# Sharing PSUM pairs between the Vh tiles, and placing the rank-32 additions ahead of the layer-norm statistics

## The chip, the cores and the metric

The kernel runs on one core of a Trainium2 chip. The metric is the device time of one execution in microseconds (us). Five engines work side by side, each through its own queue of instructions in order: TensorE (PE, matrix products, with the weight loads listed apart as PEld), VectorE (DVE), ScalarE (ACT), GpSimd (POOL) and SyncE (SP), which issues the DMAs. They meet through semaphores. PE writes into PSUM, the accumulation memory of eight banks; the other engines read it from there.

## The reference

Eight batches of attention with a feature-wise softmax, a gated MLP on top of it (`_moe_ref`), then a second one that mixes along the sequence at rank 32 and along the channels (`_moe2_ref`):

```python
# q_s, k_s: softmax of q over the features, of k over the sequence
kv = np.einsum('bhsd,bhse->bhde', k_s, v)
x = np.einsum('bhsd,bhde->bhse', q_s, kv)          # [8, 576, 512] after the transpose
h = gelu(x @ w_in); u, v = h[..., :512], h[..., 512:]
v_n = (v - mean(v)) / np.sqrt(var(v) + 1e-06) * g_ln
v_s = np.einsum('ts,bsd->btd', w_sg, v_n) + b_sg[None, :, None]
x = x + (u * v_s) @ w_out
...
h = xt @ U @ V                                     # rank 32, xt is x transposed
u = x + h.transpose(0, 2, 1)
out = u + np.maximum(u @ w_ch1, 0.0) @ w_ch2
```

## The kernel before

Products are made from a high and a low part of each operand (names ending in `h` and `l`; the low part is made by a subtraction that the helper `low` puts on DVE or POOL, and all subtractions and additions of that kind bear line L55). The helper `mm` (L52) issues all matrix products. The program has a loop over eight batches b = 0 to 7 and then, from 631.9 us of the span on, a long phase of channel products (tiles `mm`) which is PE from end to end and which the change doesn't touch.

One batch goes through these stages, in PE's order:

- **Vh.** Five tiles `pv` (`emit_Vh`): four of 12 matmuls and 128 rows, and tile 4 with 8 matmuls and 64 rows. ACT applies GELU to each into a buffer `ge` (three buffers), DVE makes `bn_stats` and `bn_aggr` (`stats`), POOL raises the variance to the power -1/2. `emit_ln` then makes a shift `sh` on DVE (L620), applies it on ACT (L623, `ge<-ge,sh,mv`), copies it to `vh` on ACT, and makes the low part `vl` on POOL; for tile 4 the low part is made on DVE, into the other half of the tile `vh4`.
- Between these tiles stand products of the batch before: transposes of its result (`emit_yT`, tile `pt`), the rank-32 product with U (`emit_U`, `pp`), and the rank-32 additions (`emit_PV`: tiles `pw`, added on DVE as `yt<-pw,yt`, and sent out by SP as `u2d<-yt`).
- **Uh.** Four tiles `pu` (`emit_Uh`), to each of which ACT applies GELU (L645, `ut<-pu`). The buffer of `ut` is that of `yt`, so the first `ut` waits for the four `u2d` transfers. Beside this DVE and ACT prepare the softmax of the next batch: on DVE `q_sub` (`qt<-qt,qm`), `k_sub` (`kt<-kt,pb`), then `q_sum` and `q_norm`; on ACT the exponentials (L458 for q, L439 for k). The exponential and GELU need different function tables, and an `ACT_TABLE_LOAD` stands wherever ACT goes from one to the other.
- **S.** Four tiles `pS` (`emit_S`): the first needs `vh4` at its end. DVE makes `gt<-pS,gl,bb` (L665) and `gt<-gt,ut`; `split_G` makes `gh` and `gl`.
- **pk, pt, y, px.** The product `pk` of keys and values, transposes of q (`emit_qT`, low part `ql` on DVE), the output product `py` (`emit_y`, which needs all four `gt` and, by its PSUM buffers, the reads of `gt` and `ql`), and `px`, the x of the next batch.

PSUM is shared by two pools: `big`, three buffers of two banks each, and `ps1`, two buffers of one bank each. In the kernel before each `pv` takes a whole `big` buffer though it fills one bank, as do the tiles `pw`, the transposes of tiles 2 and 3 of the batch before, `pu`, `pS`, `py` and `px`.

PE's order and, inside the batches, DVE's order are those in which the code is written (`in_order`). ACT, POOL and SP are put in order by a scheduler when the program is built. `slot` puts work on the weights of the later phase (`chw`, `f`, `stg`) at fixed places. A wait for a tile is a wait for the whole tile: two halves of one tile are one thing to those waits when their reader and the next writer are different engines.

Of the kernel before, what the change touches and what calls it, by code (L numbers as in the profile page):

```python
# [8 lines left out]
F32 = mybir.dt.float32  # L9
# [3 lines left out]
ALU = mybir.AluOpType  # L13
# [9 lines left out]
def fused_kernel(tc, q, k, v, w_in, g_ln, w_sgT, b_sg, w_out, U, V, w_ch1, w_ch2, outT):  # L23
    nc = tc.nc
    B, S, C = q.shape
    P = 128
    H, D = 8, 64
    NT = S // P
    R = S - NT * P
    NC = C // P  # L30
    F = w_out.shape[0]
# [17 lines left out]
    pe, act, dve, pool, sp = nc.tensor, nc.scalar, nc.vector, nc.gpsimd, nc.sync  # L49

    def mm(out, lhsT, rhs, first, last, onto=False):
        pe.matmul(out, lhsT, rhs, start=first, stop=last, skip_group_check=onto)  # L52

    def tt(eng, out, a, b, op):
        return eng.tensor_tensor(out=out, in0=a, in1=b, op=op)  # L55
# [4 lines left out]
    def copy(out, src):  # L60
        return act.activation(out, src, AF.Copy)  # L61

    def low(eng, out, src, hi):
        return tt(eng, out, src, as_f32(hi), ALU.subtract)

    def opened(name, bufs=1, **kw):
        cm = tc.tile_pool(name=name, bufs=bufs, reuse_waits="tile", **kw)
        return cm.__enter__(), lambda: cm.__exit__(None, None, None)
# [8 lines left out]
    ps2, close_ps2 = opened("ps2", 3, space=PSUM)  # L77
    ps1, close_ps1 = opened("ps1", 2, space=PSUM)
# [4 lines left out]
    wrk, close_wrk = opened("wrk", side="left")  # L83
    wo_p, close_wo = opened("wo_p", side="left")
    sg_p, close_sg = opened("sg_p", side="left")
    tmpp, close_tmpp = opened("tmpp", 2, side="left")
# [10 lines left out]
    half = cst.tile([P, 1], F32, name="half")  # L97
# [326 lines left out]
    def k_spread(b):  # L424

        mx = kx_t[b]
        pb = ps1.tile([P, NC, P], F32, tag="ps1", name="pb")
        for c in range(NC):
            pe.transpose(pb[:, c], mx[:, c : c + 1].to_broadcast([P, P]), ident)
        kx_t[b] = pb.rearrange("p c e -> p (c e)")  # L430
# [15 lines left out]
    def q_max(b, t):  # L446
        if t == 0:
            q_s[b] = tmpp.tile([P, NT + 1, H], F32, tag="qm", name="qm")
        dve.tensor_reduce(
            out=q_s[b][0 : TR[t], t], in_=q3(t), op=ALU.max, axis=mybir.AxisListType.X  # L450
        )
# [79 lines left out]
    def halves(t):  # L531
        return t[:, :, 0:HS]

    def two(ap):
        return ap.rearrange("p (j n) -> p j n", n=HS)
# [10 lines left out]
    def behind(eng):  # L546
        return tc.issue_after(last[eng].ins)
# [31 lines left out]

    vh = {}  # L580
    ln = {}

    def emit_Vh(b, t):
        xh, xl, xr, _ = x_t[b]
        pv = ps2.tile([P, 1024], F32, tag="big", name="pv")[:, 0:F]
        wv_h, wv_l = wi[1]
        for kc in range(NC):
            if t < NT:
                a, l = xh[:, kc, t * P : (t + 1) * P], xl[:, kc, t * P : (t + 1) * P]
                mm(pv, a, wv_h[:, kc], kc == 0, False)  # L590
                mm(pv, a, wv_l[:, kc], False, False)
                mm(pv, l, wv_h[:, kc], False, kc == NC - 1)
            else:
                a = xr[:, kc].rearrange("p j r -> p (j r)")
                mm(pv, a, wv_h[:, kc], kc == 0, False)
                mm(pv, a, wv_l[:, kc], False, kc == NC - 1)
        ge = tmpp.tile([P, F], F32, tag="ge", name="ge", bufs=3)
        ln[b, t] = ge
        if t < NT:
            act.activation(ge, pv, AF.Gelu_apprx_tanh)  # L600
        else:
            copy(ge[0:R], pv[64 : 64 + R])
            tt(dve, ge[0:R], pv[0:R], ge[0:R], ALU.add)
            act.activation(ge[0:R], ge[0:R], AF.Gelu_apprx_tanh)
# [11 lines left out]
    def emit_ln(b, t):  # L616
        ge, mv = ln.pop((b, t))
        n = TR[t]
        shift = tmpp.tile([P, 1], F32, tag="sh", name="sh", bufs=4)
        dve.scalar_tensor_tensor(  # L620
            out=shift[0:n], in0=mv[0:n, 0:1], scalar=-1.0, in1=mv[0:n, 1:2], op0=ALU.mult, op1=ALU.mult
        )
        act.activation(ge[0:n], ge[0:n], AF.Identity, bias=shift[0:n], scale=mv[0:n, 1:2])  # L623
        h = wrk.tile([P, F], F32R, tag=f"vh{t}", name=f"vh{t}")
        if t < NT:
            l = wrk.tile([P, F], F32R, tag=f"vl{t}", name=f"vl{t}")
            copy(h, ge)
            low(pool, l, ge, h)
            vh[b, t] = (h, l)
        else:  # L630
            copy(h[0:R], ge[0:R])
            low(dve, h[64 : 64 + R], ge[0:R], h[0:R])
            vh[b, t] = h
# [57 lines left out]
    def emit_yT(b, t):  # L691
        n = TR[t]
        if t not in (2, 3) or b == B - 1:
            pt = ps1.tile([P, C], F32, tag="ps1", name="pt1")
        else:
            pt = ps2.tile([P, 1024], F32, tag="big", name="pt1")[:, 0:C]
        for c in range(NC):
            pe.transpose(pt[0:n, c * P : (c + 1) * P], y_t[b][:, c, t * P : t * P + n], ident)  # L698
        h = wrk.tile([P, C], F32R, tag=f"vh{t}", name=f"yh{t}")
        if t < NT:  # L700
            l = wrk.tile([P, C], F32R, tag=f"vl{t}", name=f"yl{t}")
            copy(h, pt)
            low(dve, l, pt, h)
            yn[b, t] = (h, l)
        else:
            copy(h[0:R], pt[0:R])
            low(dve, h[64 : 64 + R], pt[0:R], h[0:R])
            yn[b, t] = (h,)
# [31 lines left out]
    def emit_PV(b, c):  # L740
        s = pu_t[b][:, c * P : (c + 1) * P]
        pw = ps2.tile([P, 2, 512], F32, tag="big", name="pw")
        for j in range(2):
            mm(pw[:, j, 0:HS], s, v_w[:, j * HS : (j + 1) * HS], True, True)
        y = y_t[b][:, c]
        tt(dve, two(y), halves(pw), two(y), ALU.add)
        sp.dma_start(u2d[:, c, :, b * HS : (b + 1) * HS].rearrange("j p n -> p j n"), two(y))
# [26 lines left out]
    def u_parts(g, kc):  # L774

        n, t0 = GROUPS[g], starts[g]
        if kc == 0:
            parts = [tmpp.tile([P, F], F32, tag="ge", name="us", bufs=3) for _ in range(3)]
            parts.append(wrk.tile([P, F], F32, tag="xr", name="us3"))
        else:  # L780
            parts = [wrk.tile([P, F], F32, tag=x, name="us") for x in ("vh0", "vl0", "vh1", "vl1")]
        parts = [t[:, 0:n] for t in parts]
        for x, t in enumerate(parts):
            sp.dma_start(t, u2d[x % 2, kc + 2 * (x // 2), :, t0 : t0 + n])
        return parts
# [103 lines left out]
    us = {}  # L889
# [364 lines left out]
    for b in range(B):  # L1254
# [12 lines left out]
            load_ahead()  # L1267
        for t in range(NT + 1):
            emit_Vh(b, t)
            if nxt:  # L1270
                with behind(dve):
                    for t2 in Q_MAX[b > 0][t]:
                        q_max(nxt, t2)
                    for _ in range(FOLDS[b > 0][t]):
                        next(fold)
            if t < NT:
                stats(b, t)
            slot(TURNS[b][0][t])
            if t > 0:
                emit_ln(b, t - 1)  # L1280
            if t == NT:
                stats(b, t)
            if b > 0:
                for t2 in ((2,), (3, 4), (), (), ())[t]:
                    emit_yT(b - 1, t2)
            if t == 2 and b > 0:
                for t2 in range(NT + 1):
                    emit_U(b - 1, t2)
            if b > 0:
                for c in ((), (), (), (0, 1), (2, 3))[t]:  # L1290
                    emit_PV(b - 1, c)

        spread_at = 2 if b else 3
        if nxt:
# [13 lines left out]
        for f in range(NF):  # L1308
            if nxt and f == spread_at:
                k_spread(nxt)  # L1310
            if b == 0:
                slot(TURNS[b][1][f])
            if not nxt:
                for _ in range((0, 2, 2, 2)[f]):
                    next(prep, None)
            emit_Uh(b, f)
            if f == 0:
                emit_ln(b, NT)
                if nxt:
                    load_v(nxt)  # L1320
                else:
                    next(prep, None)
            if nxt:
                for t in Q_SUB[b > 0][f]:
                    q_sub(nxt, t, pool if t in Q_SUB_POOL[b > 0] else dve)
                for t in K_SUB[b > 0][f]:
                    if f >= spread_at:
                        k_sub(nxt, t)
                    else:
                        late_k.append(t)  # L1330
                if f == spread_at:
                    for t in late_k:
                        k_sub(nxt, t)
            if b > 0:
                slot(TURNS[b][1][f])
# [181 lines left out]
```

## Time and profile before

| | |
|---|---|
| times of three runs | 1308.29, 1314.53 and 1307.48 us, median 1308.29 |
| the profiled execution | 1311.05 us, of which the span is 1309.2 us |
| mean granted TensorE clock | 0.991 |
| PE busy | 1260.0 us, 96% |
| DVE busy | 969.0 us, 74% |
| ACT busy | 636.9 us, 49% |
| POOL busy | 330.4 us, 25% |
| chain that ended last | PE 79%, DVE 7%, DMA 4%, ACT 2% |

A busy share is an average over the whole span. The stages differ: the batches 1 to 6 take some 69 to 73 us each, the first and the last batch 116 and 97 us, and the phase behind them 677 us. In a row of the timeline a bracket at the end, such as [0.21 <-ACT ge L600], is the idle time of that engine just before the row and what ended it. Successive instructions of one kind are one row with xN, and their time is that of all of them.

### The profile page before, as it was taken

The numbers are of one execution on the slowest core, as the hardware profiler recorded it, in microseconds if no ns is written. First come the engines' busy times: TensorE is split into PE (matmuls) and PEld (weight loads), VectorE is DVE, ScalarE is ACT, GpSimd is POOL, SyncE is SP. The second block draws the span as 40 slices with busy tenths as digits, with TensorE's granted clock in tenths as the row PEclk, the third lists the DMA queues.
The fourth block names the chain that finished last, engine by engine and source line by source line (L and its number), as shares of the span: only waits on it lengthen the run. The fifth ranks groups of instructions, "written<-read, shape, count | busy, mean of one in ns | idle before, by whom it ended". The sixth has DMA issues, their size and how long they took to land.

```text
span 1309.2 us, 20581 instructions
## 1 busy us (share of the span) xinstructions
PE 1260.0 (96%) x7592; PEld 1139.1 (87%) x7592; DVE 969.0 (74%) x1406; ACT 636.9 (49%) x979; POOL 330.4 (25%) x426
## 2 busy tenths in 40 slices
PE   4799999999999999898999999999999999999998
PEld 3598999999898989798888888888888889999998
DVE  7888879787988888788668953598337963694485
ACT  4756656575757466654454512444134422451342
POOL 4634152624243333665340202000010002000000
PEclk9899999999999999998999999999999999999999
DMA  8515171725343352468998667678756788899896
GB/s 268 164 47 171 37 218 37 225 70 167 96 151 120 111 168 73 162 208 299 312 344 315 227 231 257 209 242 290 257 193 226 243 285 297 269 304 315 260 290 215
DMA packets 135907, 274.14 MB, mean 209 GB/s; under 512 B 15232, under 2 KB 56704, under 8 KB 135808
## 3 DMA queue, kind: packets, MB, share of 16 engines
q1 hardware_dynamic: 135808, 272.84, 63.2%
q8 instruction: 60, 0.98, 0.3%
q14 instruction: 39, 0.32, 0.1%
HBM read 224.56 MB, written 48.23 MB: 208 GB/s over the span
## 4 chain that ended last, share of the span: by engine, by line
PE 79%; DVE 7%; DMA 4%; ACT 2%; issue 1%; POOL 1%; SPq 0%; DVEq 0%; ACTq 0%; POOLq 0%
PE mm L52 50%; PE pS L52 6%; PE pu L52 6%; PE pv L52 5%; PE py L52 5%; DMA stg<-in_w_ch_dram 1%; PE pm L52 1%; PE pp L52 1%; PE px L52 1%; PE pt L698 1%; DVE yt L55 1%; DVE f L183 1%; PE pk L52 1%; PE pt L527 1%; DMA wu<-wd 1%
## 5 line engine op out<-in xcount | busy, mean ns | idle before, releaser
L52 PE MATMUL mm<-oh,wu 128*128 128x512 f32 (+1 forms) x1120 | 320.7, 367 | 0.0
L52 PE MATMUL mm<-uh,wu 128*128 128x512 f32 (+1 forms) x1064 | 303.7, 366 | 1.9 <-DMA wu<-wd 1.1
L52 PEld LDWEIGHTS mm<-oh,wu 128*128 128x128 f32 x1120 | 207.0, 188 | 26.1
L52 PEld LDWEIGHTS mm<-uh,wu 128*128 128x128 f32 x1064 | 196.3, 188 | 26.4 <-issue 1.4
L52 PE MATMUL mm<-ol,wu 128*128 128x512 f32 (+1 forms) x560 | 205.7, 367 | 0.0
L61 ACT ACTIVATE oh<-h 128x1024 fp32r<-128x1024 f32 (+1 forms) x140 | 135.2, 973 | 124.8 <-PE mm L52 102.4
L52 PE MATMUL mm<-ul,wu 128*128 128x512 f32 (+1 forms) x532 | 194.9, 366 | 0.0
L55 DVE TENSOR_TENSOR ol<-h,oh 128x1024 fp32r<-128x1024 f32 (+1 forms) x140 | 155.4, 1113 | 40.9 <-ACT oh L61 40.1
L55 POOL TENSOR_TENSOR ust<-ust 128x1024 f32<-128x1024 f32 (+1 forms) x16 | 36.4, 2282 | 389.4 <-DMA ust<-u2d 348.8
L55 DVE TENSOR_TENSOR h<-mm,u 128x1024 f32<-128x1024 f32 (+1 forms) x57 | 63.3, 1111 | 87.8 <-PE mm L52 87.7
L52 PEld LDWEIGHTS mm<-ol,wu 128*128 128x128 f32 x560 | 105.2, 188 | 13.1
L55 DVE TENSOR_TENSOR u<-mm,u 128x1024 f32<-128x1024 f32 (+1 forms) x53 | 58.9, 1111 | 76.7 <-PE mm L52 71.3
L52 PEld LDWEIGHTS mm<-ul,wu 128*128 128x128 f32 x532 | 99.9, 188 | 12.1
L55 POOL TENSOR_TENSOR chw<-f,chw 128x256 fp32r<-128x256 f32 x98 | 78.9, 820 | 95.4 <-ACT chw L61 95.3
L55 DVE TENSOR_TENSOR h<-h,h 128x1024 f32<-128x1024 f32 (+1 forms) x80 | 88.9, 1112 | 0.0
L1041 ACT ACTIVATE h<-mm 128x1024 f32<-128x1024 f32 (+1 forms) x19 | 17.8, 938 | 130.8 <-PE mm L52 130.8
L1032 ACT ACTIVATE h<-h 128x1024 f32<-128x1024 f32 (+1 forms) x60 | 58.1, 969 | 33.9 <-DVE h L55 33.9
L61 ACT ACTIVATE chw<-f 128x256 fp32r<-128x256 f32 x112 | 42.6, 412 | 62.7 <-DVE f L184 23.1
L61 ACT ACTIVATE u<-mm 128x1024 f32<-128x1024 f32 (+1 forms) x24 | 22.5, 939 | 103.1 <-PE mm L52 86.9
L171 POOL TENSOR_SCALAR stg<-stg 128x256 f32<-128x256 f32 (+1 forms) x83 | 41.0, 496 | 99.7 <-DMA stg<-in_w_ch_dram 39.0
L52 PE MATMUL py<-gh,wo_h 128*128 128x288 f32 x256 | 57.6, 307 | 3.0 <-DVE gt L665 2.1
L52 PE MATMUL py<-gl,wo_h 128*128 128x288 f32 x256 | 56.0, 301 | 3.4 <-DVE gl L55 3.4
(165 smaller groups left out, 2650.2 us busy)
## 6 DMA issues: line engine op xcount, KB each, us to landing
wu<-wd SPq DMA_DIRECT2D x280, 512.0 KB, 4.4
wd<-chw SPq DMA_DIRECT2D x112, 256.0 KB, 3.6
stg<-in_w_ch_dram SPq DMA_DIRECT2D x64, 256.0 KB, 3.7
u2d<-yt SPq DMA_DIRECT2D x32, 288.0 KB, 2.4
vt<-in_v_dram SPq DMA_DIRECT2D x32, 256.0 KB, 6.7
qt<-in_q_dram SPq DMA_DIRECT2D x7, 1024.0 KB, 8.1
kt<-in_k_dram SPq DMA_DIRECT2D x7, 1024.0 KB, 6.1
res<-u2d SPq DMA_DIRECT2D x12, 512.0 KB, 5.3
```

The lines of the kernel that those rows point to most:

```text
L52: pe.matmul(out, lhsT, rhs, start=first, stop=last, skip_group_check=onto)
L55: return eng.tensor_tensor(out=out, in0=a, in1=b, op=op)
L61: return act.activation(out, src, AF.Copy)
L171: eng.tensor_scalar(out=hi, in0=hi, scalar1=F64_MOST, scalar2=-F64_MOST, op0=ALU.min, op1=ALU.max)
L183: dve.tensor_scalar(out=b, in0=b, scalar1=3, scalar2=None, op0=ALU.logical_shift_left)
L527: pe.transpose(pt[:, t * P : (t + 1) * P], qt[:, t, c * P : (c + 1) * P], ident)
L698: pe.transpose(pt[0:n, c * P : (c + 1) * P], y_t[b][:, c, t * P : t * P + n], ident)
L1032: act.activation(h, h, AF.Relu)
L1041: act.activation(h_out(j, 11, n), bank, AF.Relu)
```

## The change

From batch 1 on the tiles `pv` 0 and 1 share one `big` buffer, one bank each, and so do 2 and 3 (`half_pair`). Tile 4 takes a buffer of `ps1`. The transposes of tiles 2 and 3 of the batch before share one as well. The GELU is taken out of `emit_Vh` into `gelu_Vh`, so that from tile 3 on the rank-32 additions of the batch before (`emit_PV`) are written ahead of the GELU and the statistics of that tile. The shift `sh` becomes a `tensor_scalar` whose scalar is a pointer to the variance term. The layer norm of tile 4 is written behind Uh 1 in place of Uh 0. In the preparation of the last phase two buffers change places.

```diff
+    def half_pair(key, half, name):
+        if half == 0:
+            banks[key] = ps2.tile([P, 2, 512], F32, tag="big", name=name)
+        return banks[key][:, half]
 
     def emit_Vh(b, t):
-        pv = ps2.tile([P, 1024], F32, tag="big", name="pv")[:, 0:F]
+        if b == 0:
+            pv = ps2.tile([P, 1024], F32, tag="big", name="pv")[:, 0:F]
+        elif t < NT:
+            pv = half_pair("pv", t % 2, "pv")
+        else:
+            pv = ps1.tile([P, C], F32, tag="ps1", name="pv")
...
+    def gelu_Vh(b, t):
+        pv = ln[b, t]
...
     def emit_ln(b, t):
-        dve.scalar_tensor_tensor(
-            out=shift[0:n], in0=mv[0:n, 0:1], scalar=-1.0, in1=mv[0:n, 1:2], op0=ALU.mult, op1=ALU.mult
+        dve.tensor_scalar(
+            out=shift[0:n], in0=mv[0:n, 0:1], scalar1=mv[0:n, 1:2], scalar2=-1.0, op0=ALU.mult, op1=ALU.mult
...
     def emit_yT(b, t):
-            pt = ps2.tile([P, 1024], F32, tag="big", name="pt1")[:, 0:C]
+            pt = half_pair("yt", t % 2, "pt1")
...
-            parts = [tmpp.tile([P, F], F32, tag="ge", name="us", bufs=3) for _ in range(3)]
-            parts.append(wrk.tile([P, F], F32, tag="xr", name="us3"))
+            parts = [tmpp.tile([P, F], F32, tag="ge", name="us", bufs=3) for _ in range(2)]
+            parts.append(wrk.tile([P, F], F32, tag="xr", name="us2"))
+            parts.append(tmpp.tile([P, F], F32, tag="ge", name="us", bufs=3))
...
             emit_Vh(b, t)
+            if b == 0 or t < 3:
+                gelu_Vh(b, t)
...
+            if b > 0 and t >= 3:
+                for c in ((0, 1), (2, 3))[t - 3]:
+                    emit_PV(b - 1, c)
+                gelu_Vh(b, t)
             if t < NT:
                 stats(b, t)
...
-            if b > 0:
-                for c in ((), (), (), (0, 1), (2, 3))[t]:
-                    emit_PV(b - 1, c)
...
             emit_Uh(b, f)
             if f == 0:
-                emit_ln(b, NT)
...
+            if f == 1:
+                emit_ln(b, NT)
```

PE's order of products stays as it was. On ACT, the order that the scheduler makes changes in every batch. In the Uh stage of batch 4 ACT has, before (`ge<-ge,sh,mv 64x512` and `vh_4195` are the layer norm of tile 4, the `ut` are the GELUs of Uh, L458 is the exponential of q):

```order
L61 ACTIVATE vh_4138<-ge 128x512
L623 ACTIVATE ge<-ge,sh,mv 64x512
L61 ACTIVATE vh_4195<-ge 64x512
L645 ACTIVATE ut<-pu 128x576 x2
L458 ACT_TABLE_LOAD
L458 ACTIVATE qt<-qt 128x512 x2
L177 ACTIVATE f_4572<-stg 128x256
L458 ACTIVATE qt<-qt 128x512 x2
L645 ACT_TABLE_LOAD
L645 ACTIVATE ut<-pu 128x576
```

and with the change, in the same place (L660 is the old L645, L638 the old L623):

```order
L61 ACTIVATE vh_4136<-ge 128x512
L660 ACTIVATE ut<-pu 128x576
L458 ACT_TABLE_LOAD
L458 ACTIVATE qt<-qt 128x512 x2
L177 ACTIVATE f_4560<-stg 128x256
L660 ACT_TABLE_LOAD
L660 ACTIVATE ut<-pu 128x576
L638 ACTIVATE ge<-ge,sh,mv 64x512
L61 ACTIVATE vh_4223<-ge 64x512
L660 ACTIVATE ut<-pu 128x576
L458 ACT_TABLE_LOAD
```

The layer norm of tile 4 moved from ahead of both `ut` to behind the second, with two table loads, two exponentials and a step of the weight preparation ahead of it. In the whole program ACT has 30 table loads before and 50 with the change.

At the beginning of the same batch ACT has, before (`x` and `yh` are copies, `ge<-pv` is the GELU of Vh 0):

```order
L61 ACTIVATE yh_3945<-pt_3940 128x512
L61 ACTIVATE x_3888<-px 128x576
L600 ACTIVATE ge<-pv 128x512
L61 ACTIVATE yh_3987<-pt_3982 128x512
L600 ACTIVATE ge<-pv 128x512
```

and with the change:

```order
L61 ACTIVATE yh_3936<-pt_3931 128x512
L61 ACTIVATE x_3879<-px 128x576
L615 ACT_TABLE_LOAD
L615 ACTIVATE ge<-pv 128x512
L61 ACTIVATE yh_3978<-pt_3973 128x512
L615 ACTIVATE ge<-pv 128x512
```

A table load has come ahead of the first GELU; before, batches 0, 1 and 5 alone have one there, and with the change all of them. On PE the first product of Vh 1 waits for that GELU, since it writes the other half of the tile which the GELU reads.

DVE in the Uh stage of batch 4 has, before:

```order
L55 TENSOR_TENSOR yt<-pw,yt 128x576 x2
L421 TENSOR_REDUCE mx<-pm 128x4
L620 SCALAR_TENSOR_TENSOR sh<-mv 64x1
L55 TENSOR_TENSOR vh_4195<-ge,vh_4195 64x512
L55 TENSOR_TENSOR qt<-qt,qm 128x512 x2
L55 TENSOR_TENSOR chw<-f_3551,chw 128x256
L55 TENSOR_TENSOR qt<-qt,qm 128x512 x2
```

and with the change:

```order
L421 TENSOR_REDUCE mx<-pm 128x4
L55 TENSOR_TENSOR qt<-qt,qm 128x512 x2
L55 TENSOR_TENSOR chw<-f_3542,chw 128x256
L635 TENSOR_SCALAR sh<-mv 64x1
L55 TENSOR_TENSOR vh_4223<-ge,vh_4223 64x512
L55 TENSOR_TENSOR qt<-qt,qm 128x512 x2
L55 TENSOR_TENSOR qt<-qt,qm 64x512
```

Two `q_sub` and a `chw` have come ahead of the low part of `vh4`, and the additions to `yt` have left this place for one further up, ahead of the statistics of tile 4.

## Rows read from the trace of the kernel before

**Rows 1.** Stages: from:to, length, then busy (count) of PE, PEld, DVE, ACT, POOL.

```profile
323.50:392.60 69.10, 68.75 (x531) 64.55 (x530) 60.18 (x113) 43.52 (x74) 23.31 (x29) 1.00 0.40 129
...
631.90:1309.20 677.30, 671.50 (x3276) 595.65 (x3276) 439.55 (x429) 258.86 (x298) 61.01 (x51) 1.00 0.80 266
```

**Rows 2.** Timeline, PE at the end of Vh, batch 4: start, length, engine, instruction, idle.

```profile
338.11 0.69 PE L52 MATMUL pw<-v_w,pst 128*128 128x288 f32 x4
...
339.01 0.50 PE L52 MATMUL pv<-wih,xr 128*128 128x512 f32 x1 [0.21 <-ACT ge L600]
...
341.00 1.20 PE L52 MATMUL pw<-v_w,pst 128*128 128x288 f32 x4
...
342.60 0.53 PE L52 MATMUL pu<-xh,wih 128*128 128x288 f32 x2
```

**Rows 3.** Timeline, the first GELU and the start of Vh 1, batch 4.

```profile
326.54 0.60 ACT L600 ACTIVATE ge<-pv 128x512 f32<-128x512 f32 x1 [0.78 <-PE pv L52]
...
326.69 0.48 PE L52 MATMUL pv<-wih,xh 128*128 128x512 f32 x1
```

**Rows 4.** Timeline, the same place in batch 1.

```profile
118.42 1.28 ACT L600 ACT_TABLE_LOAD   x1
119.71 0.60 ACT L600 ACTIVATE ge<-pv 128x512 f32<-128x512 f32 x1
...
118.70 0.48 PE L52 MATMUL pv<-wih,xh 128*128 128x512 f32 x1
```

**Rows 5.** Timeline, all engines in the Uh stage of batch 4.

```profile
342.47 1.27 DVE L620 SCALAR_TENSOR_TENSOR sh<-mv 128x1 f32<-128x1 f32 x1
...
345.38 1.30 POOL L55 TENSOR_TENSOR vl<-ge,vh 128x512 fp32r<-128x512 f32 x1
...
346.75 0.82 ACT L623 ACTIVATE ge<-ge,sh,mv 64x512 f32<-64x512 f32 x1 [1.50 <-DVE sh L620]
...
348.26 0.69 DVE L55 TENSOR_TENSOR vh<-ge,vh 64x512 fp32r<-64x512 f32 x1 [1.55 <-ACT vh L61]
...
348.50 1.43 ACT L645 ACTIVATE ut<-pu 128x576 f32<-128x576 f32 x2 [0.27 <-DMA u2d<-yt]
...
348.98 1.29 DVE L55 TENSOR_TENSOR qt<-qt,qm 128x512 f32<-128x512 f32 x2
...
351.24 1.15 ACT L458 ACTIVATE qt<-qt 128x512 f32<-128x512 f32 x2
...
355.91 0.43 PE L52 MATMUL pS<-sg_h,vh 128*128 128x288 f32 x2
```

**Rows 6.** Timeline, DVE and PE from the last gt to py, batch 4.

```profile
371.02 0.82 DVE L665 SCALAR_TENSOR_TENSOR gt<-pS,gl,bb 128x576 f32<-128x576 f32 x1 [0.25 <-PE pS L52]
...
375.08 1.42 DVE L55 TENSOR_TENSOR ql<-pt,qh 128x576 fp32r<-128x576 f32 x2
...
374.46 0.51 PE L52 MATMUL py<-gh,wo_h 128*128 128x288 f32 x2
```

**Rows 7.** Timeline, the same place in batch 2 (first row) and batch 5.

```profile
232.88 0.82 DVE L665 SCALAR_TENSOR_TENSOR gt<-pS,gl,bb 128x576 f32<-128x576 f32 x1 [1.98 <-PE pS L52]
...
436.36 0.82 DVE L665 SCALAR_TENSOR_TENSOR gt<-pS,gl,bb 128x576 f32<-128x576 f32 x1 [1.12 <-PE pS L52]
...
440.09 0.82 DVE L665 SCALAR_TENSOR_TENSOR gt<-pS,gl,bb 128x576 f32<-128x576 f32 x1 [0.68 <-PE pS L52]
...
446.05 1.42 DVE L55 TENSOR_TENSOR ql<-pt,qh 128x576 fp32r<-128x576 f32 x2
...
446.85 0.53 PE L52 MATMUL py<-gh,wo_h 128*128 128x288 f32 x2
```

**Rows 8.** Timeline, DVE in the Uh stage of batch 0.

```profile
71.18 0.69 DVE L55 TENSOR_TENSOR vh<-ge,vh 64x512 fp32r<-64x512 f32 x1 [2.26 <-ACT vh L61]
```

**Rows 9.** Timeline, two waits of batch 7, PE's and DVE's.

```profile
554.64 1.29 PE L52 MATMUL pw<-v_w,pst 128*128 128x288 f32 x4 [1.84 <-DVE yt L55]
...
568.45 0.69 DVE L55 TENSOR_TENSOR ul<-us,uh 128x512 fp32r<-128x512 f32 x1 [2.78 <-ACT uh L61]
```

More of the change, by code (lines that the diff above doesn't have):

```diff
@@ L581, in fused_kernel @@
     ln = {}
+    banks = {}
+    def half_pair(key, half, name):
+        if half == 0:
+            banks[key] = ps2.tile([P, 2, 512], F32, tag="big", name=name)
+        return banks[key][:, half]
     def emit_Vh(b, t):
         xh, xl, xr, _ = x_t[b]
-        pv = ps2.tile([P, 1024], F32, tag="big", name="pv")[:, 0:F]
+        if b == 0:
[4 more added lines that the diff above has]
+            pv = ps1.tile([P, C], F32, tag="ps1", name="pv")
+        ln[b, t] = pv
         wv_h, wv_l = wi[1]
```

## The prediction, written before the change was run

> **What bounds the kernel now.** I read the table of stages first. In a batch from the middle PE is busy 68.75 of 69.10 us, and in the long phase behind the batches 671.50 of 677.30 [rows 1]. So PE sets the time everywhere. The change leaves PE's order and the number of its products alone; it can only take out waits of PE, or add some. The last phase isn't touched and is costed at nothing. I then read the timeline of PE in batch 4 for its gaps, and for each gap the bracket that names the releaser, and after that ACT and DVE for the work that PE waits for later.
>
> **What is removed.** Three waits at the end of Vh, in batch 4. (1) Vh 4 waits until the GELU of Vh 3 has given a `big` buffer back: PE idles 0.21 us, and its first product takes 0.50 in place of the usual 0.39 [rows 2]; with the refill of the pipe I take 0.35. With the change tile 4 has a buffer of `ps1` and waits for nothing recent. (2) The second pair of additions waits for DVE's first addition: its four products take 1.20 us, against 0.69 for the first pair, which waits for nothing [rows 2]. That is 0.51. With the change DVE adds before it makes the statistics. (3) Uh 0 waits for the `ge` addition of tile 4, and later for the addition that frees its buffer, which comes earlier now. No row separates this; between 0 and 0.4 us, I take 0.25. Sum 1.1 us a batch, and 6.6 for batches 1 to 6.
>
> **What is added at Vh 1.** Vh 0 and Vh 1 now share a tile, so Vh 1 can't start before the GELU of Vh 0 has read it. Before, Vh 1 started at 326.69 while that GELU ran from 326.54 to 327.14 [rows 3]. That alone is 0.45 us. But the order of ACT puts a table load ahead of this GELU. ACT was free at 326.54 - 0.78 = 325.76 [rows 3]. A load takes 1.28 us and the GELU behind it starts at once [rows 4]; so the GELU ends at 325.76 + 1.28 + 0.60 = 327.64 and PE stands still for 0.95 us. In batch 1 the load is there already: the GELU ends at 120.31, Vh 1 started at 118.70, so the wait is 1.6 us [rows 4]. I count three batches like the one (2, 4, 5) and three like the other (1, 3, 6, where copies or weight steps of ACT end late): 3 x 0.95 + 3 x 1.6 = 7.65. The bounds are 6 x 0.45 = 2.7, if the loads find room earlier, and 6 x 1.6 = 9.6. What PE waits here isn't hidden by anything: PE is what bounds the stage.
>
> The Trainium skill (ScalarE: Activation LUTs, section What ACT_TABLE_LOAD costs) states that each change of table takes about 1.28 us for the load and 1.38 for a drain, 2.66 in all. The load's length agrees with the row; of the drain the rows show nothing, since the GELU starts 0.01 us after the load ends [rows 4]. By that rule the six waits would grow by 1.38 each, and the sum below by an estimated 8.3 us.
>
> **What is moved in the Uh stage.** Here the layer norm of tile 4 comes later. Before, ACT began it at 346.75 and DVE's low part of `vh4` started at 348.26, having idled for 1.55 [rows 5]. Now, with PE 0.15 us earlier (0.95 - 1.1), Uh 0 starts at 342.45. A Uh takes about 3.2 us: four of them and one set of small transposes lie between 342.60 and 355.91 [rows 2, 5]. Uh 0 ends at 345.65. ACT then has a `ut` (0.7, half of the pair), a load 1.28, two exponentials 1.15, the weight step (0.4, by its 128x256 size beside the exponential's 128x512 I take two thirds), a load 1.28, a `ut` 0.7, and only then the norm 0.82 and a copy of about the same length as an exponential, 0.6. Adding up, 345.65 + 6.93 = 352.6 where nothing delays the exponentials. They need two `q_sub` on DVE, which meet the subtraction `vl` of POOL: 1.30 us long, and a shift of DVE that usually takes some 0.15 lasted 1.27 [rows 5]. Where `q_sub` is held like that the end is about 353.8. So the low part of `vh4` starts 4.3 to 5.5 us later than 348.26. Two `q_sub`, 1.29 us [rows 5], have been done ahead of it, so DVE's later chain is late by 3.0 to 4.2. I take 3.5, since the `vl` may end before. The early additions to `yt` help the start of `ut`, which waited for `u2d` at 348.50 [rows 5]; that is contained above.
>
> Does PE see it? DVE runs from there to the last `gt` almost without a gap: 0.25 us of idle before `gt` 3 [rows 6]. The second `py` needs the first `ql`, read by 375.08 + 0.71 = 375.8, and starts 3.2 us after 374.46, at 377.7 [rows 6]: 1.9 us in hand. So batch 4 loses 3.5 - 0.25 - 1.9 = 1.35. In batch 5 there are 1.12 + 0.68 us of idle, but `ql` was read by 446.76 and `py` went on at 446.85 [rows 7]: 0.1 in hand, loss 1.6. In batch 2 the idle of 1.98 [rows 7] and a margin like that of batch 4 cover the whole, loss 0. The mean of the three is 1.0; for six batches 6.0. With the bounds 3.0 and 4.2 for the lateness the three give 0.65 and 1.55 on average, so 3.9 to 9.3.
>
> **Batches 0 and 7.** In batch 0 the order of ACT changes little, and DVE idled 2.26 us before the low part of `vh4` [rows 8]; the two `q_sub` fit in. Gain 1.3, bounds 0 and 2.3. In batch 7 the wait of 1.84 [rows 9] goes, the wait at Vh 1 comes (1.6), and a buffer of the last preparation is now free only after the late `vh4`: 3.5 less the 2.78 us that DVE idled there [rows 9], 0.7. Sum +0.5, bounds -2 and +2.
>
> **The shift.** It reads one tensor and one pointer in place of two tensors. Alone it takes the same 0.15 us; held by POOL it may be freed of up to 1.1 us once a batch [rows 5]. It stands on DVE ahead of the layer norm, not ahead of PE's next wait, and the moved norm lies behind it. Costed at nothing; if it isn't hidden it gives up to 1.1 of the 3.5 back.
>
> **The sum.** -6.6 + 7.65 + 6.0 - 1.3 + 0.5 = +6.25, say +6. The profiled execution is at 1311.05 and would be at 1317; the median of the runs shown is 1308.3, so I forecast 1314.
>
> **Rivals.** (A) Faster: the later layer norm is absorbed in all batches, since only batches 4 and 5 are short of DVE time, and the loads ahead of GELU find ACT free early. Then 2.7 - 6.6 - 2.3 - 2 = -8, 1300. For it: DVE has idle time in nearly all stages. Against: the row of batch 4 [rows 6] and ACT's order, in which the load stands behind the last copy. (B) No change: the wait at Vh 1 comes as forecast, the late norm is covered: 7.65 - 6.6 - 1.3 + 0.5 = 0, 1308. (C) Slower by more: `q_sub` is held by POOL in each batch, the lateness is 4.2, and PE's margin is exhausted in all. It decides from the point where the low part of `vh4` is later than the margin and idle of its batch (2.15 us in batch 4). Then 9.6 + 9.3 - 6.6 + 1 = +13, 1321. For it: `vl` stands at the very place. Against it: the idle time of batch 2 [rows 7]. The Trainium skill (ScalarE: Activation LUTs, section Table sets: the hidden batching unit) says to do all calls of one table together; the change goes the other way, with 20 more loads. (D) A change of table holds ACT for longer than the load itself: if by once more its length, 1.28, ACT would be late by that at Vh 1 and by twice that in the Uh stage of six batches, +6 + 7.7 + 15.4 = +29, 1337. Against it stands the GELU that starts at once [rows 4]; I leave it 2 in 100. With the drain of 1.38 us that the Trainium skill gives (ScalarE: Activation LUTs, What ACT_TABLE_LOAD costs) it would be an estimated +31.
>
> **How the numbers follow.** What a measurement of this kernel can tell from no change is about 0.5%, 6.5 us. The forecast has 0.45, of which 0.27 lie within 0.5% and 0.18 above; (A) 0.15, faster; (B) 0.15, within; (C) 0.23 and (D) 0.02, slower. Faster 0.15, same 0.42, slower 0.43. The range leaves out most of (A) and the far end of (C) and (D): 1301 to 1322.
>
> **What would show it.** Right: a PE gap of 0.9 to 1.6 us ahead of Vh 1 in each batch from 1 on, ended by ACT's GELU; no gap ahead of Vh 4; the second four `pw` in about 0.7 us; the low part of `vh4` about 4 us behind where it stood; and `py` or `S` waiting for DVE in the batches 3 to 6. Wrong: if the batches 1 to 6 become shorter than 69 us, the wait at Vh 1 is smaller or DVE has more room than I read; if the long phase changes, something else was at work.

## The result and the profile after

The changed kernel took 1328.17 us (median of four runs, 1327.96 to 1328.42), against 1308.53 before: a ratio of 1.0143, with a 95% interval of 1.0127 to 1.0159. A second measurement on another occasion gave 1323.94 us, a ratio of 1.0102 (1.0087 to 1.0118). The kernel became slower by 14 to 20 us. The forecast was 1314, with a range up to 1322; the direction was right, and both measurements lie above the range.

The page of the changed kernel: the span, the busy time of each engine with its share of the span, and the chain of work that ended last, by engine.

```profile
span 1326.5 us, 20642 instructions
...
PE 1261.1 (95%) x7592; PEld 1140.0 (86%) x7592; DVE 967.6 (73%) x1406; ACT 663.4 (50%) x999; POOL 333.8 (25%) x426
...
PE 65%; DVE 17%; ACT 8%; DMA 5%; issue 2%; POOL 2%; SPq 1%; DVEq 0%; POOLq 0%; ACTq 0%
```

PE's work is what it was (1260.0 us before). ACT has 26.5 us more, of which 20 table loads of 1.28 make 25.6. The chain tells the rest: DVE had 7% of it and ACT 2% before, now 17% and 8%. Which waits these are, the list of PE's waits between 115 and 653 us shows (what waited, for what, us in total, times, the longest). Before:

```profile
PE py L52 <- DVE gl L55: 3.4, 2, 2.9
...
PE pw L52 <- DVE yt L55: 1.8, 1, 1.8
PE pv L52 <- ACT ge L600: 1.3, 6, 0.2
```

And after:

```profile
PE py L52 <- DVE gl L55: 8.5, 3, 4.1
PE pv L52 <- ACT ge L615: 6.8, 7, 1.5
PE py L52 <- DVE ql L55: 3.3, 5, 1.8
PE pt L713 <- DVE yl L55: 2.5, 2, 2.2
PE py L52 <- ACT chw L61: 2.1, 2, 1.8
PE pt L527 <- DVE yt L55: 1.3, 1, 1.3
PE pS L52 <- DVE gt L680: 1.2, 1, 1.2
```

The second row is the wait at Vh 1. Nearly all the others stand at `py` and behind it, where PE waits for DVE. That holds for the row of `chw` too: `chw` is no input of `py`, and both of its waits end within 0.2 us behind a `gt` of DVE, which `py` needs for its PSUM buffer.

To see where the time went I took from each timeline the start of the first product of each stage; the difference of two neighbours is the length of a stage. In the following table, Vh is from the first `pv` to the first `pu`, and "pk to px" is from the first `pk` to the first `px`. Both, and the whole of a batch, are sums over batches 1 to 6. The last two columns are batch 7 from its first `pv` to the first `mm`, and the long phase from there to the end of the span.

| trace | Vh | S | pk to px | batches 1-6 | batch 0 | batch 7 | long phase |
|---|---|---|---|---|---|---|---|
| before | 115.7 | 91.1 | 106.3 | 417.8 | 79.0 | 98.7 | 677.3 |
| after | 116.6 | 90.0 | 117.3 | 428.6 | 78.0 | 102.2 | 680.5 |
| after, second trace | 118.3 | 90.0 | 115.7 | 428.6 | 77.1 | 102.3 | 677.0 |

Uh (79.8 to 79.9) and the stage from `px` to the next Vh (24.7 to 24.8) are alike in all three. So the loss has two places that both traces show: 9 to 11 us between `pk` and `px` in batches 1 to 6, and 3.5 us in batch 7. The long phase is longer in the first trace alone. S is shorter by 1.1 us, all of it in batch 6. Vh, where the change was to gain, lost 0.9 to 2.6.

**Vh 1.** The timeline of the changed kernel in batch 4, the row of ACT and of PE that answer to [rows 3]:

```profile
329.01 0.75 ACT L61 ACTIVATE x<-px 128x576 f32<-128x576 f32 x1
329.78 1.28 ACT L615 ACT_TABLE_LOAD   x1
331.07 0.60 ACT L615 ACTIVATE ge<-pv 128x512 f32<-128x512 f32 x1
...
331.72 0.50 PE L52 MATMUL pv<-wih,xh 128*128 128x512 f32 x1 [0.76 <-ACT ge L615]
```

The load begins when the last copy ends and the GELU when the load ends; PE starts 0.05 us behind the GELU and was idle for 0.76. There is no room in which a drain could be. At the end of the same Vh, the rows that answer to [rows 2]:

```profile
343.17 0.69 PE L52 MATMUL pw<-v_w,pst 128*128 128x288 f32 x4
343.70 0.40 PE L52 MATMUL pv<-wih,xr 128*128 128x512 f32 x1
...
345.57 0.70 PE L52 MATMUL pw<-v_w,pst 128*128 128x288 f32 x4
...
346.46 0.51 PE L52 MATMUL pu<-xh,wih 128*128 128x288 f32 x2
```

No bracket is left: Vh 4 follows at once, and the second four `pw` take 0.70 in place of 1.20.

**The norm of tile 4.** ACT and DVE in the Uh stage of batch 4, answering to [rows 5]:

```profile
352.43 1.24 ACT L458 ACTIVATE qt<-qt 128x512 f32<-128x512 f32 x2 [0.31 <-DVE qt L55]
353.56 0.42 ACT L177 ACTIVATE f<-stg 128x256 f32<-128x256 f32 x1
354.00 1.28 ACT L660 ACT_TABLE_LOAD   x1
355.30 0.65 ACT L660 ACTIVATE ut<-pu 128x576 f32<-128x576 f32 x1
355.84 0.81 ACT L638 ACTIVATE ge<-ge,sh,mv 64x512 f32<-64x512 f32 x1
...
350.40 2.60 DVE L55 TENSOR_TENSOR qt<-qt,qm 128x512 f32<-128x512 f32 x2
...
357.34 0.69 DVE L55 TENSOR_TENSOR vh<-ge,vh 64x512 fp32r<-64x512 f32 x1 [3.89 <-ACT vh L61]
```

Uh 0 began at 346.46, so the low part of `vh4` stands 10.9 us behind it; before it was 5.7. DVE idled for 3.89 us in front of it. The two `q_sub` took 2.60 us where they took 1.29 before [rows 5]. In the other five of the batches 1 to 6 the norm itself comes ahead of the second load, and only its copy to `vh`, which the low part needs, behind it (batch 3: load 280.49, norm 283.22, load 284.04, copy 285.88). The chain behind it begins with the first `q_sum`, before (first row) 12.7 us behind Uh 0 and now 16.4:

```profile
355.32 1.26 DVE L464 TENSOR_REDUCE qs<-qt 128x8 f32<-128x512 f32 x2
...
362.86 0.67 DVE L464 TENSOR_REDUCE qs<-qt 128x8 f32<-128x512 f32 x1
```

**Batch 7.** The low part of `vh4` stood 7.9 us behind Uh 0 before:

```profile
563.93 0.68 DVE L55 TENSOR_TENSOR vh<-ge,vh 64x512 fp32r<-64x512 f32 x1 [1.55 <-ACT vh L61]
```

Now it stands 14.2 behind. DVE, ACT and SP, where the buffer that the late norm frees is filled again:

```profile
577.77 1.26 DVE L55 TENSOR_TENSOR vh<-ge,vh 64x512 fp32r<-64x512 f32 x1 [2.65 <-ACT vh L61]
...
579.07 0.32 SPq L800 DMA_DIRECT2D us<-u2d  x1
...
583.30 0.63 ACT L61 ACTIVATE uh<-us 128x512 fp32r<-128x512 f32 x1 [4.04 <-DMA us<-u2d]
...
583.35 0.69 DVE L55 TENSOR_TENSOR us<-us 128x512 f32<-128x512 f32 x1 [3.59 <-issue]
...
588.04 0.81 DVE L680 SCALAR_TENSOR_TENSOR gt<-pS,gl,bb 128x576 f32<-128x576 f32 x1
```

The transfer is issued 0.04 us after the low part of `vh4` ends, its data is there 4.2 us later, and only then DVE goes on; the first `gt` stands behind it in DVE's order.

### The profile page after: what moved, and what is told of

The parts are those of the page before. It is cut to its first block, busy times and chain, and to the rows that moved or that the text cites. A ratio compares the mean times of both kernels' runs of the same rounds, so it can differ in the third digit from the quotient of the medians.

```text
span 1326.5 us, 20642 instructions
## 1 busy us (share of the span) xinstructions
PE 1261.1 (95%) x7592; PEld 1140.0 (86%) x7592; DVE 967.6 (73%) x1406; ACT 663.4 (50%) x999; POOL 333.8 (25%) x426
## 4 chain that ended last, share of the span: by engine, by line
PE 65%; DVE 17%; ACT 8%; DMA 5%; issue 2%; POOL 2%; SPq 1%; DVEq 0%; POOLq 0%; ACTq 0%
PE mm L52 50%; PE pv L52 5%; PE py L52 3%; DVE qt L55 3%; PE pu L52 2%; DMA stg<-in_w_ch_dram 2%; DVE qs L464 1%; DVE gt L680 1%; DVE yt L55 1%; DVE f L183 1%; PE pp L52 1%; ACT xh L61 1%; DVE gl L55 1%; ACT x L61 1%; DVE kt L55 1%
```

## The experiments

Two theories stood against each other. **L**: the late layer norm is what costs. **P**: the shared pairs cost, at Vh 1 and by what they shift. The ratios are to the kernel before on the same chip. Sums of stages are as in the table above.

**ln_back** takes the late norm out of the change, and the exchange of the two buffers that goes with it.

```diff
             if f == 0:
+                emit_ln(b, NT)
...
-            if f == 1:
-                emit_ln(b, NT)
```

> The changed kernel with the layer norm of tile 4 back behind Uh 0 (and the buffers of the last preparation as before); shared pairs, early additions and the new shift stay. Theory L (most of the loss is the late layer norm: about 10 us in batches 1 to 6 and 6.5 in batch 7): 1308 to 1314 us. Rival P (the loss comes from the shared pair at Vh 1 and what it shifts): it stays at 1322 or above. In the profile theory L expects the low part of vh4 about 6 us behind the start of Uh 0 in place of 10 to 11, and py without waits for DVE beyond 0.3 us a batch.

1308.11 us, ratio 0.999 (0.998 to 0.9999). The stage from `pk` to `px` is back at 106.0 us and batch 7 at 96.8; Vh is unchanged at 116.8. So the whole loss goes with the place of the norm, 1328.2 - 1308.1 = 20 us (16 from the second measurement), and the pairs' theory falls. That 20 holds the 3.5 us of the long phase, which are not shown to belong to the change (after_again, below).

**ln_only** is the reverse: the kernel before with the late norm alone.

> The kernel before with nothing changed but the place of the layer norm of tile 4 (behind Uh 1) and the two buffers of the last preparation that go with it. Theory L: +14 to +18 us on before, 1322 to 1327. Rival P: within 5 us of before, 1313 at most.

1316.79 us, ratio 1.0058 (1.0042 to 1.0074): +7.6, between the two. The norm costs about half as much without the rest of the change, or less. In its trace the first `ut` comes 7 to 9 us behind Uh 0, behind two table loads and two exponentials, and in five of six batches ACT does the norm ahead of it, at 5.8 to 6.1, against 6.9 to 9.4 with the whole change. ACT in batch 3 (Uh 0 at 274.44):

```profile
277.12 1.28 ACT L458 ACT_TABLE_LOAD   x1
279.14 1.24 ACT L458 ACTIVATE qt<-qt 128x512 f32<-128x512 f32 x2 [0.74 <-DVE qt L55]
280.28 0.80 ACT L623 ACTIVATE ge<-ge,sh,mv 64x512 f32<-64x512 f32 x1
281.10 1.28 ACT L645 ACT_TABLE_LOAD   x1
282.39 1.20 ACT L645 ACTIVATE ut<-pu 128x576 f32<-128x576 f32 x2
283.47 0.62 ACT L61 ACTIVATE vh<-ge 64x512 fp32r<-64x512 f32 x1
```

The `q_sum` chain starts at 15.2 to 15.5 in five of them, against 15.8 to 16.5. With the whole change the first `ut` comes 3.7 to 4.7 us behind Uh 0, ahead of the first load and the norm. That the early additions, meant as a gain, bring it forward so and push the norm back is likely but not shown apart. Batch 7 takes 99.8 in ln_only, against 102.2.

**ln_back_b7** puts the norm back in the last batch only, and with it the two buffers of the last preparation.

```diff
+                if not nxt:
+                    emit_ln(b, NT)
...
-            if f == 1:
+            if nxt and f == 1:
                 emit_ln(b, NT)
```

> The changed kernel with the layer norm of tile 4 back behind Uh 0 in the last batch alone, with the buffers of the last preparation as before. Theory L says that in the last batch the late norm frees a buffer late, whose DMA of 4.2 us DVE then waits for: 1328 - 6.5 = 1321.5 us, with the last batch near 96 us from Vh to the channel products in place of 102. Rival (the last batch is late since DVE and POOL are late anyway): less than 2 us of gain, 1326 or above.

1318.54 us, ratio 1.007 (1.0049 to 1.0091). Batch 7 takes 95.0 us in place of 102.2, and batches 1 to 6 stay at 428.3: 7.2 us for the last batch alone. In ln_back, whose last batch is written the same way, it took 96.8, so the last batch is worth 5.4 to 7.2. The time fell by 9.6 us against the first measurement and by 5.4 against the second; the difference is in the parts that also differ between two traces of the changed kernel (below). Norm and buffers move together here: that the refill costs, and not the late norm by itself, is read from the rows above and was not tested apart.

**after_act** leaves the change and pins one thing on ACT: the exponentials of q come behind the copy that ends the norm.

```diff
-            with contextlib.nullcontext() if b else tc.issue_after(last['g', 3].ins):
+            with tc.issue_after(last['vh4'].ins) if b else tc.issue_after(last['g', 3].ins):
                 for t in range(NT + 1):
                     q_exp(nxt, t)
```

> The changed kernel as it is (pairs, early additions, layer norm of tile 4 written behind Uh 1), with one thing pinned: on ACT the exponentials of q come behind the copy that ends that layer norm, in batches 1 to 6, so that no table load and no exponential stands ahead of it. If it is ACT's order that makes the norm late (theory A), the low part of vh4 starts some 7 to 8 us behind Uh 0 in place of 10.2 to 11.0, the stage from pk to px loses at most 2 us in six batches in place of 11, and the time is 1318 to 1320. If it is DVE's own order (two q_sub ahead of the norm), it stays at 1326 or above. Batch 7 and the last phase are not touched by it and should stay at 102 and 680 us.

1312.24 us, ratio 1.0018 (1.0009 to 1.0028), a larger gain than expected. In batch 4 the same places as above read, on ACT and DVE:

```profile
349.23 0.63 ACT L660 ACTIVATE ut<-pu 128x576 f32<-128x576 f32 x1
349.76 0.80 ACT L638 ACTIVATE ge<-ge,sh,mv 64x512 f32<-64x512 f32 x1
350.60 0.63 ACT L61 ACTIVATE vh<-ge 64x512 fp32r<-64x512 f32 x1
351.25 1.28 ACT L458 ACT_TABLE_LOAD   x1
...
351.26 0.69 DVE L55 TENSOR_TENSOR vh<-ge,vh 64x512 fp32r<-64x512 f32 x1 [2.28 <-ACT vh L61]
```

The low part of `vh4` is at 9.3 us behind Uh 0 (341.98) here, at 8.4 to 8.6 in the other batches, later than the 7 to 8 that were expected. The later chain (first `q_sum`) is late by 1.5 to 2.1 us against before, and the stage from `pk` to `px` takes 106.0 us: nothing is lost. Batch 7 stays at 101.9. So it is ACT's order, loads and exponentials ahead of the norm, that costs in batches 1 to 6, and DVE's chain has at least those 1.5 to 2.1 us in hand in each of them.

**no_pair** gives the Vh tiles and transposes their own buffers and keeps the rest.

```diff
-            pv = half_pair("pv", t % 2, "pv")
+            pv = ps2.tile([P, 1024], F32, tag="big", name="pv")[:, 0:F]
...
-            pt = half_pair("yt", t % 2, "pt1")
+            pt = ps2.tile([P, 1024], F32, tag="big", name="pt1")[:, 0:C]
```

> The changed kernel with each Vh tile 0 to 3 and each transpose of tiles 2 and 3 in a big buffer of its own again; tile 4 stays in a one-bank buffer, and the rest stays as changed. PE then has no wait for GELU at Vh 1 (6.8 us in seven batches). Theory L: what PE gains at Vh 1 remains gained, 1328 - 6.8 = 1321 us, or up to 1325 where the later stages are bound by DVE and take a part back. Rival P: 1312 or less, since the pairs are the cause.

1323.67 us, ratio 1.0112 (1.0093 to 1.0131). Vh falls from 116.6 to 110.8, 17.9 us in batches 1, 2 and 4; the gain of 4.5 is what theory L had expected. It is less than the 5.8 of Vh, and the last batch takes 104.1 there.

**no_pair_ln_back** takes out both pairs and late norm.

> Of the change only the early rank-32 additions, the one-bank buffer of Vh tile 4 and the new shift: no shared pairs, and the layer norm of tile 4 behind Uh 0 as before. From the stages of the runs so far: Vh of 17.9 us in place of 19.15 in batches 1 to 6 (-7.4), batch 7 shorter by 2 to 3, batch 0 by 1 to 2: 1297 to 1300 us, faster than both kernels. Rival (the end of the batch is bound by DVE and ACT and takes the gain back): 1306 or above.

1303.67 us, ratio 0.9961 (0.9948 to 0.9973), 4 us above what was expected. Batches 1 to 6 did what was expected (Vh 107.6, all six 408.8), but batch 7 takes 98.8, and batch 0 78.3.

**pair_pin** is ln_back with the GELU of Uh 3 held back behind the last exponential of k, so that no table load stands ahead of the first GELU of Vh.

```diff
...
+        if 0 < b < B - 1 and f == 3:
+            last['pu'] = pu
+            return
...
-                k_exp(nxt)
+                ke = k_exp(nxt)
+            if b:
+                with tc.issue_after(ke.ins):
+                    act.activation(two(u_t[b][:, 3]), halves(last['pu']), AF.Gelu_apprx_tanh)
```

> The shared pairs stay, the layer norm of tile 4 is behind Uh 0, and the GELU of Uh 3 is held back behind the last exponential of k in batches 1 to 6, so that no table load stands ahead of the first GELU of Vh. If the load makes up half of the wait at Vh 1, as forecast (0.45 us without it against 0.95 to 1.6 with it), Vh takes 18.3 to 18.5 us in batches 1 to 6 in place of 19.0 to 20.2, and the time is about 4 us below the kernel with the load (1308.1): 1303 to 1305. Rival (the wait is for the pair alone): Vh stays at 19.0 and more, 1308. A wait of S 2 for the GELU of Uh 3 would be a cost of its own, at most 1 us a batch.

1301.92 us, ratio 0.9944 (0.9928 to 0.9959). PE's wait at Vh 1 in batch 4 is now

```profile
327.69 0.50 PE L52 MATMUL pv<-wih,xh 128*128 128x512 f32 x1 [0.25 <-ACT ge L616]
```

in place of 0.76, and Vh takes 18.4 us in batches 3, 4 and 5 (19.0 to 19.6 with the load, 17.9 without pairs). So a pair costs about 0.5 us there, and the load in front of it another 0.6 to 1.1. In batches 1, 2 and 6 Vh stays at 19.2 to 19.6, against the 18.3 to 18.5 expected.

**before_pin** and **pv_pin** use the same pin where there are no pairs: on the kernel before, and on no_pair_ln_back.

> The kernel before with the GELU of Uh 3 held back behind the last exponential of k in batches 1 to 6, two table loads fewer in all. Nothing waits for a table load there but what has room: within 2 us of before, 1307 to 1311. If loads on ACT set the time by themselves (2 x 1.28 us): 1306.5.

> The early additions without pairs, layer norm behind Uh 0, and the GELU of Uh 3 behind the last exponential of k, so that 28 table loads stand in place of 40. Where the loads ahead of the first GELU are hidden without pairs, this is the same as without the pin, 1297 to 1300; if they cost something there too, it is 2 to 4 us less. Rival: S 2 waits for the later GELU of Uh 3, up to 1 us in each of six batches, 1303.

1309.24 us, ratio 1.0004 (0.9995 to 1.0013), and 1304.77 us, ratio 0.9969 (0.9958 to 0.998), against 0.9961 without the pin. Where nothing waits for the first GELU, no cost of the loads shows: 28 of them are as good as 40.

**sh_only** is the kernel before with the new shift alone.

> The kernel before with the shift as a tensor_scalar with a pointer, nothing else. Forecast: hidden, within 1.5 us of before; in the profile the 40 shifts take 6 to 10 us in all in place of 18.4, because those beside a POOL subtraction are no longer held. Rival (the held shifts are on the path): 3 us less or more.

1306.58 us, ratio 0.9969 (0.9957 to 0.9981), 3.3 us less: the rival's case, not the forecast's. The groups of the shift in both traces (busy us, mean ns, idle before), before and then here:

```profile
L620 DVE SCALAR_TENSOR_TENSOR sh<-mv 128x1 f32<-128x1 f32 (+1 forms) x40 | 18.4, 461 | 2.3 <-POOL mv L55 2.3
```

```profile
L620 DVE TENSOR_SCALAR sh<-mv 128x1 f32<-128x1 f32 (+1 forms) x40 | 8.1, 202 | 2.2 <-POOL mv L55 2.2
```

None of the 40 is held any more (194 to 208 ns each, against 138 to 2741). Batch 0 takes 77.4 us (79.0 before), batch 6 70.1 (71.5), batch 7 95.5 (98.7); the others gain nothing. Over all runs, batch 0 takes 76.9 to 78.3 with the new shift and 78.7 to 79.0 with the old one.

**hybrid** and **hybrid_pin** keep the pairs in the last batch alone, to find a version better than both kernels.

> Early additions and the one-bank buffer for tile 4 in batches 1 to 7, shared pairs in the last batch alone, layer norm of tile 4 behind Uh 0. By the stages of the runs so far: Vh of 17.9 us in batches 1 to 6 as without pairs, and batch 7 at 95 to 97 us as with pairs, in place of 98.8: 1300 to 1302, faster than before and than the same without any pairs (1303.7). Rival (batch 7 is longer for another reason than the pairs): 1303 to 1305.

> The same with the GELU of Uh 3 behind the last exponential of k, 28 table loads. Where loads are hidden once nothing waits for the first GELU: the same time, 1300 to 1302. Rival (freed ACT time helps): 1297 to 1299.

1303.59 us, ratio 0.994 (0.9928 to 0.9953), and 1303.28, ratio 0.9946 (0.9934 to 0.9959). The expected gain did not come: batch 7 takes 97.9 and 98.3, near the 98.8 without any pairs, so the pairs were not what makes the last batch long or short.

**best** keeps the early additions and the one-bank buffer of tile 4 in batches 1 to 6, the new shift everywhere, and leaves the last batch as it was before. Against the changed kernel, at the place of the early additions:

```diff
...
-            if b > 0 and t >= 3:
+            if 0 < b < B - 1 and t >= 3:
...
```

> Early additions, one-bank buffer of tile 4 in batches 1 to 6 alone, the new shift in all, no shared pairs, layer norm of tile 4 behind Uh 0; the last batch in its old form. If PE's gain at Vh is lost again in the last batch (which waits for DVE at py), the batches 1 to 6 take 67.9 us each but for batch 6, the last one 95.5 as with the new shift alone, and the time is 1297 to 1300. Rival (the early additions gain in the last batch as well): 1302 to 1304.

1300.30 us, ratio 0.9927 (0.9913 to 0.9942): 9.6 us less than before and the lowest ratio of all, though its interval overlaps those of pair_pin, hybrid and hybrid_pin. Batches 1 to 6 take 408.8 us, the last one 95.0, near the 95.5 of sh_only. PE starts Uh 0 of the last batch later than in hybrid (21.8 us behind the first `pv` against 19.7), and reaches the long phase 2.9 us sooner: in hybrid `py` waited 6.3 us for DVE, here 3.4.

**after_again** is the changed kernel a second time.

> The changed kernel once more, unaltered. If the long phase and the dropped clock of batch 5 belong to the change, it again shows about 680 us from the first channel product on, a wait of 2 us and more for a weight transfer there, and 17 us from py to px in batch 5; if they are chance, 676 to 679 us and about 16 us, with the time at 1325 to 1328.

1323.94 us, as told above, below the 1325 to 1328 expected for chance. Batches 1 to 6 and batch 7 are the same to 0.1 us as sums (within batches 1 to 6, Vh is 1.7 longer and `pk` to `px` 1.7 shorter). The long phase is 677.0, as before, so the 3.5 us of the first trace are not shown to belong to the change. They have a place in that trace, a wait of PE for a transfer of weights:

```profile
1111.98 0.59 PE L52 MATMUL mm<-uh,wu 128*128 128x384 f32 x2 [2.73 <-DMA wu<-wd]
```

The like wait was 1.07 us before and 0.34 in the second trace. Behind it the granted clock of the 3.4 us from 1113.2 was 0.50; in the other two traces the clock does not fall there. Why the transfer came late isn't shown. Batch 5 shows no fall of the clock in the second trace; that fall cost about 1.4 us in the first, but it doesn't part the two times, since batches 1 to 6 take 428.6 us in both. Why four runs of the first occasion all had about 1328 isn't settled.

## Why the prediction was wrong, point by point

- **What is removed** (1.1 us a batch): right. Vh without pairs takes 17.9 us against 19.15, so 1.2. The part at Vh 4 and at the additions shows in the rows above.
- **The wait at Vh 1** (0.95 and 1.6): right in the main. Vh takes 19.0 in batches 2, 4 and 5 and 19.6 in 1 and 3, against 17.9 without pairs: 1.1 and 1.7. Batch 6 takes 20.5, and in the second trace batches 1, 5 and 6 take 20.0, 19.7 and 21.2. The split between pair and load (0.45 and the rest) is that of pair_pin. Gain and wait nearly cancel, as the sum had it: Vh +0.9 us over six batches (+2.6 in the second trace), forecast 7.65 - 6.6.
- **The lateness of the norm**: right. Low part of `vh4` 4.6 to 5.4 us later behind Uh 0 (forecast 4.3 to 5.5), the chain behind it 3.4 to 4.2 later (forecast 3.0 to 4.2, 3.5 taken). The `q_sub` were held, as the upper end had it.
- **What PE sees of it**: wrong in size. Forecast 6.0 over six batches, measured 9.4 and 11.0 from `pk` to `px`. For batches 4 and 5 the step held (1.2 and, in the trace without the fall of the clock, 1.9, against 1.35 and 1.6). It failed in batch 2, where I set 1.98 us of idle plus a margin like that of batch 4 against the lateness and got zero; measured 1.5 to 1.7. The idle ahead of one `gt` is used up there, but further on PE's transposes of q wait for a `big` buffer that DVE's addition to `yt` has to read first, a consumer that I had not looked at:

```profile
247.61 0.75 DVE L55 TENSOR_TENSOR yt<-py,x 128x576 f32<-128x576 f32 x1
...
248.42 0.76 PE L527 MATMUL pt<-ident,qt 128*128 128x128 f32 x5 [1.27 <-DVE yt L55]
```

With 1.6 in place of that zero the mean of the three is 1.5 and the six batches 9. No batch had the 3.9 us in hand that I gave to batch 2: lateness less loss is 1.6 to 2.8 us in the six batches of the second trace, and in after_act a lateness of 1.5 to 2.1 cost nothing. Lateness minus 2, six times, is 10.
- **Batch 7**: wrong. Forecast +0.5, bounds -2 and +2; measured +3.5 both times, and 5.4 to 7.2 for the norm with its buffers. The stages ahead gained more than the forecast had: Vh is 3.1 us shorter, Uh 1.2, with a wait at Vh 1 of 0.41 in place of 1.6. The loss behind them, forecast 0.7, was about 7.7. I set the lateness of batch 4 (3.5) against an idle of 2.78 [rows 9]. But the norm was 6.3 us later there (14.2 behind Uh 0 against 7.9), and what it frees is only then filled, by a transfer that takes 4.2 us and stands ahead of the first `gt`. I had named the buffer and not added its DMA, and had taken the lateness of another batch.
- **Batch 0**: -1.0 and -1.9, forecast -1.3, for another reason. ln_only gives -0.3; sh_only gives -1.6. It goes with the shift.
- **The shift** (nothing): wrong. Alone it gives 3.3 us, in batches 0, 6 and 7; I had only looked at batch 4, where nothing is gained by it.
- **The long phase** (nothing): in the second trace right; in the first it was 3.2 us longer, by a wait for a transfer and a fall of the clock behind it (after_again), of which the cause is open.

The sum missed its size by the two terms that hang on the late norm: 3 to 5 us in batches 1 to 6 and 3 in batch 7, and in the first measurement by up to 6 more that the second doesn't show. Of the rivals, C came nearest: the margin exhausted in all batches. Its 1321 left batch 7 too low and the wait at Vh 1 too high. D, a longer hold of ACT at each load, is not what happened: the rows of Vh 1 leave no room for it.

## What to carry to other kernels

When a step is moved on one in-order engine, lay out the order that a scheduler then makes on the other engines too: here the end of a norm that was moved by one stage fell behind two table loads and two exponentials, and that cost more than all that the change gained. Here the late step cost about its lateness less the smallest margin of all consumers down the line, not of the first, and a buffer that it frees came late by its refill as well. Changes that are bundled are worth taking apart: three of the five parts here, kept where they help, make the kernel 0.7% faster, and the bundle made it 1.0 to 1.4% slower.

## What the runs showed of the hardware

A shift with two tensors, on 64x1 or 128x1 elements, took up to 2.74 us where POOL ran subtractions and additions beside it (the longest, from 559.64, ended 0.01 us behind the last of four of them); with one tensor and a pointer none of the 40 took more than 0.21, and its length where nothing held it rose from 0.15 to 0.20 us. And a wait of PE was at times followed by a fall of its clock: in the first trace, after 1.81 us of idle in batch 5, the granted clock of the 2.9 us from 454.6 was 0.50, the lower level of 1.2 GHz, and six pairs of products took the length of this row

```profile
455.66 0.68 PE L52 MATMUL py<-gh,wo_l 128*128 128x288 f32 x2
```

in place of 0.42. In the second trace PE idled 1.83 us at the same place, and the clock of the same stretch was 1.00. What decides it isn't shown.
